# Loading 3 of the 32 rows of B's output weights second, by transfers of 119 and 9 partitions, and storing A's result by one transfer

## The chip, the cores and the metric

The kernel runs on one core of one Trainium2 chip. The metric is the device time of one execution in microseconds. Before the change the median of 3 runs is 825.41 us (825.28 to 825.46).

## What is computed

Two decode steps of attention with a key-value cache, A and B, are computed side by side and their outputs are set one behind the other. Each has one token, 32 heads of 128 and caches of 16384 positions in bfloat16. A attends to all positions, B only to the last 4096.

```python
W = min(4096, max(256, Sk // 4))                       # B only: window of the cache
q = (x @ wq).reshape(B, Sq, Hq, Dh).transpose(0, 2, 1, 3)
scores = einsum("bhqd,bhkd->bhqk", q, k) * Dh ** -0.5
p = softmax(scores, axis=-1)
o = einsum("bhqk,bhkd->bhqd", p, v)
out = o.transpose(0, 2, 1, 3).reshape(B, Sq, Hq * Dh) @ wo      # wo: 4096 x 512
# result: concatenate([out of A, out of B], axis=-1): 1 x 1 x 1024
```

Nearly all of the work is reading: the page counts 352.32 MB read from HBM, of which the two `wo` are 4 MB each.

## The kernel before, in words

**Tiles and order.** The caches are read in 20 tiles: 16 of A (two heads each, 128 partitions x 64 KB for keys and as much for values) and 4 of B (eight heads each, read as two halves of 32 KB a partition). A list `steps` (L94 to L101) puts B's tiles at T = 0, 7, 13 and 19. Keys go through a ring of two buffers (`kslot`), values through one buffer (`vslot`). For each tile VectorE multiplies the keys by the query (`scores_prod`, L206) and adds up along the head dimension (`scores_tree`, L212 and L216), ScalarE takes the exponentials (`soft`), TensorE multiplies by the values (`pv`, L272) and folds the result into a sum (`fold`, L288). The order is written out by hand (`manual_schedule`).

**Queues.** All large loads are issued by SyncE (SP), in program order, on one DMA queue (q1 in the profile). One such transfer of 128 partitions leaves 128 data packets, one a partition, and 16 packets of 4 bytes in the trace: each of the 16 DMA engines moves 8 partitions and then counts the transfer's semaphore up. Each engine works through its packets in the order of issue. SP also waits: before an issue it waits for the buffer to be free and, for some, for an older transfer to have landed.

**The end of the kernel.** In the last pass of the main loop (T = 19) the loads are the last values of B (`vlast`, two halves, L414 and L122) and then the two output weights (`load_wo`, L139 to L144), into the buffer `wot`: A's `wo` by one transfer, B's by five, of 16, 8, 4, 3 and 1 rows (`wo_pieces`, L368). A "row" here is one of the 32 rows of 512 numbers (1 KB) that each partition holds, so that a piece of n rows is 128 packets of n KB, and the pieces are 2048, 1024, 512, 384 and 128 KB.

TensorE then multiplies A's attention output by A's `wo` (`project_a`, L336), sums the groups (`finish_a`, L346), and ScalarE stores A's 512 numbers in two transfers (L350). `project_b` (L352 to L366) takes B's 32 rows in their order, r = 0 to 31, by four matmuls of 128 columns each (L357); every piece has a semaphore of its own, so the matmuls of a row wait until the piece that holds it has landed on all engines. When row 31 is done, VectorE copies the sums to `rows_b` (L362) and ScalarE and SP store them by four transfers (L364). Nothing is behind that but the end of the program.

Of the kernel before, what the change touches and what calls it, by code (L numbers as in the profile page):

```python
# [11 lines left out]
P = 128  # L12
# [4 lines left out]
HQ, DH = 32, 128  # L17
# [8 lines left out]
def kernel(  # L26
# [14 lines left out]
    nc = tc.nc  # L41
# [4 lines left out]
    DN = A_wo.shape[1]  # L46
# [16 lines left out]
    def kslot(name):  # L63
        return kring.tile([P, 2 * CH, DH], BF16, tag="kring", name=name)

    def vslot(name):
        return vring.tile([P, 2 * CH, DH], BF16, tag="vring", name=name)
# [7 lines left out]
    A, B = _Side(), _Side()  # L75
# [31 lines left out]
    def flat(t):  # L107
        return t.rearrange("p l d -> p (l d)")
# [15 lines left out]
    def new_k(T):  # L124
        K[T] = kslot("kt")

    def load_k(T, parts=(0, 1)):
        load(T, A_k_cache, B_k_cache, K[T], parts)

    def load_v(T, t):  # L130
        V[T] = t
        load(T, A_v_cache, B_v_cache, t)

    def load_wq(s):
        nc.sync.dma_start(  # L135
            out=s.wq_t.rearrange("p (c f) -> p c f", c=KC), in_=s.wq.rearrange("(p c) f -> p c f", c=KC)
        )

    def load_wo(s, pieces):  # L139
        src = s.wo.rearrange("(p r) f -> p r f", r=HQ)  # L140
        r = 0
        for n in pieces:
            nc.sync.dma_start(out=s.wo_t[:, r : r + n, :], in_=src[:, r : r + n, :])
            r += n  # L144

    def make_masks(s):
        nc.vector.tensor_reduce(out=s.mask[:, :], in_=by_head(s, identf[:, :]), axis=AX.X, op=ALU.add)
        z = QR - s.rows
        nc.vector.memset(s.fold[:, :], 0.0)
        nc.vector.tensor_reduce(  # L150
            out=s.fold[:, z : z + s.rows],
            in_=identf[:, :].rearrange("p (g x) -> p x g", g=NG)[:, 0 : s.rows, :], axis=AX.X, op=ALU.add,
        )

    def turn_x(xrow):
        ps = ps_t.tile([P, KC, 2], F32, tag="tp", name="xps")
        xr = xrow[:, :].rearrange("s (p c) -> s c p", c=KC)
        for c in range(KC):
            nc.tensor.matmul(ps[:, c, :], lhsT=xr[:, c, :], rhs=two_b[:, :], start=True, stop=True)
        for s in (B, A):  # L160
            nc.vector.tensor_copy(s.xT[:, :], ps[:, :, s.k])

    def clear_x(s, t):
        s.xb = t[:, 0 : s.nh * KC * P].rearrange("p (h c m) -> p h c m", h=s.nh, c=KC)
        nc.vector.memset(s.xb, 0.0)

    def spread_x(s):
        for j in range(s.nh):
            dst = s.xb[:, j, :, :]
            if s is A:  # L170
                dst = dst.rearrange("p c (h i) -> p c h i", h=s.nh)[:, :, j, :]
            else:
                dst = dst.rearrange("p c (i h) -> p c i h", h=s.nh)[:, :, :, j]
            nc.vector.tensor_copy(dst, s.xT[:, :].unsqueeze(2).broadcast_to([P, KC, P // s.nh]))

    def project_q(s):
        wq = s.wq_t.rearrange("p (c g h d) -> p c h g d", c=KC, h=s.nh, d=DH)
        for g in range(0, HQ // s.nh, 4):
            qp = ps_t.tile([P, 4, DH], F32, tag="tp", name="qp")
            n = KC * s.nh  # L180
            for k in range(n):
                c, j = divmod(k, s.nh)
                nc.tensor.matmul(  # L183
                    qp[:, :, :], lhsT=s.xb[:, j, c, :], rhs=wq[:, c, j, g : g + 4, :],
                    start=(k == 0), stop=(k == n - 1),
                )
            nc.scalar.copy(s.q[:, g : g + 4, :], qp[:, :, :])
# [14 lines left out]
    def scores_prod(T, u):  # L202
        s, g = steps[T]
        k = K[T][:, u * CH : (u + 1) * CH, :]
        j = g if s is A else 2 * g + u
        nc.vector.tensor_tensor(out=k, in0=k, in1=s.q[:, j : j + 1, :].broadcast_to([P, CH, DH]), op=ALU.mult)  # L206
# [23 lines left out]
    def max_all(T):  # L230
        un = tiles[T]
        s, U = un.s, un.s.units
        M = small.tile([2, 4], F32, tag="M", name="M")
        nc.vector.tensor_reduce(  # L234
            out=M[0:U, 0 : s.nh], in_=by_head(s, un.sm[0:U, 0:P]), axis=AX.X, op=ALU.max
        )
        Mr = one.tile([2, P], F32, tag="Mr", name="Mr")
        nc.vector.tensor_copy(  # L238
            by_head(s, Mr[0:U, :]), M[0:U, 0 : s.nh].unsqueeze(2).broadcast_to([U, s.nh, P // s.nh])
        )  # L240
        nc.tensor.transpose(un.sm[:, P : P + U], Mr[0:U, :], identf[0:U, 0:U])  # L241
# [77 lines left out]
    def own_o(s):  # L319
        s.own = square()  # L320
        pick_blocks(s.own[:, :], s.acc[:, :], DH, quad)
# [21 lines left out]
    def finish_a():  # L343
        ps = ps_m.tile([1, DN], F32, tag="sm", name="out_a")
        first = A.fold[:, QR - A.rows : QR - A.rows + 1]
        nc.tensor.matmul(ps[:, :], lhsT=first, rhs=A.wide[:, :], start=True, stop=True)  # L346
        row = one.tile([1, DN], BF16, tag="sc", name="row_a")
        nc.scalar.copy(row[:, :], ps[:, :])
        for f in range(0, DN, DN // 2):
            nc.scalar.dma_start(out=out[0, :, f : f + DN // 2], in_=row[:, f : f + DN // 2])  # L350

    def project_b():  # L352
        w = DN // NG
# [11 lines left out]
                out=out[0, :, DN + g * w : DN + (g + 1) * w], in_=rows[QR * g : QR * g + 1, :]  # L365
            )  # L366

    wo_pieces = (16, 8, 4, 3, 1)  # L368
    with tc.manual_schedule():
        xrow = one.tile([2, D], BF16, tag="pm", name="xrow")  # L370
        for s in (B, A):
            nc.scalar.dma_start(out=xrow[s.k : s.k + 1, :], in_=s.x[0, :, :])
        scratch = kslot("scratch")
        new_k(0)
        wqt = vslot("wqt")
        for k, s in enumerate((B, A)):
            s.wq_t = flat(wqt[:, k * CH : (k + 1) * CH, :])
        load_wq(B)
        load_k(0, (0,))
        load_wq(A)  # L380
        load_k(0, (1,))
        make_identity(nc, identf[:, :])
        nc.vector.tensor_copy(two_b[:, :], identf[0:2, 0:2])
        nc.vector.memset(ones[:, :], 1.0)
        nc.vector.tensor_reduce(
            out=quad[:, :], in_=identf[:, :].rearrange("p (m c) -> p c m", c=4), axis=AX.X, op=ALU.add
        )
        block = small.tile([P, P // 4], F32, tag="block", name="block", bufs=1)
        nc.vector.tensor_reduce(
            out=block[:, :], in_=identf[:, :].rearrange("p (m c) -> p m c", c=4), axis=AX.X, op=ALU.add  # L390
        )
        nc.vector.tensor_copy(
            fours[:, :].rearrange("p (m c) -> p m c", c=4), block[:, :].unsqueeze(2).broadcast_to([P, P // 4, 4])
        )
        clear_x(B, flat(scratch[:, :, :]))
        clear_x(A, one.tile([P, 2 * KC * P], BF16, tag="o4", name="xbA")[:, :])
        for o in o_banks:
            nc.vector.memset(o[:, :], 0.0)
        for s in (B, A):
            make_masks(s)  # L400
        turn_x(xrow)
        for s in (B, A):
            spread_x(s)
        project_q(B)
        project_q(A)
        new_k(1)
        load_k(1)
        for T in range(NT):
            if T >= 1:
                if T + 1 < NT:  # L410
                    new_k(T + 1)
                    load_k(T + 1)
                else:
                    load_v(T, kslot("vlast"))  # L414
            scores_prod(T, 0)
            if T >= 1:
                max_all(T - 1)
                soft(T - 1)
            scores_tree(T, 0)
            if T >= 1:  # L420
                for u in range(tiles[T - 1].s.units):
                    pv(T - 1, u)
                for u in range(tiles[T - 1].s.units):
                    fold(T - 1, u)
            if T + 1 < NT:
                load_v(T, vslot("vt"))
            else:
                wot = vslot("wot")
                for k, s in enumerate((A, B)):
                    s.wo_t = flat(wot[:, k * CH : (k + 1) * CH, :]).rearrange("p (r f) -> p r f", r=HQ)  # L430
                load_wo(A, (HQ,))
                load_wo(B, wo_pieces)
            scores_prod(T, 1)
            scores_tree(T, 1)
            tile_max(T)
        max_all(NT - 1)
        soft(NT - 1)
        normalize(A)
        own_o(A)
        pv(NT - 1, 0)  # L440
        spread_o(A)
        pv(NT - 1, 1)
        for u in range(2):
            fold(NT - 1, u)
        normalize(B)
        own_o(B)
        project_a()
        spread_o(B)
        finish_a()
        project_b()  # L450

# [29 lines left out]
```

## Time and profile before

| | |
|---|---|
| median of 3 runs | 825.41 us |
| the profiled execution: its own time | 825.65 us |
| its span (first to last instruction on the core) | 823.9 us |
| outside the span | 1.75 us |
| busy: VectorE / TensorE / ScalarE | 766.4 / 184.5 / 61.4 us |
| HBM read | 352.32 MB, 428 GB/s over the span |

The span is cut by the page into 40 slices of 20.6 us. Its row of the DMA engines' busy share shows "9", that is 90% or more, in 39 slices and "7" in the last one. Under "queue" the page lists q1 (the loads of SP and two of the last stores), q10 (ScalarE's small transfers) and two queues of kind "instruction", q8 and q14, by which the engines' own programs are read during the run. A busy share of DMA in a stretch is a mean over the 16 engines: 0.25 can be read as four of the 16 at work. The trace also keeps a record of each single packet (start, duration, size, queue); packets of one engine follow one another without a gap, which allows the 16 engines to be followed through the run.

### The profile page before, as it was taken

What the parts mean: (1) busy time and instruction counts of PE and PEld (TensorE: products, weight loads), DVE (VectorE), ACT (ScalarE), POOL (GpSimd) and SP (SyncE); (2) the same over time, 40 slices, a digit from 0 to 9 for tenths busy, and PEclk for the clock granted to TensorE, in tenths of its full rate; (3) what the DMA queues carried; (4) which work ended last, traced back from release to release, by engine and by line L of the source; (5) the groups of instructions that cost most, each with busy time, mean ns of one, the idle gap of its engine ahead of it and who ended that gap; (6) DMA issues with size and microseconds to landing.
All of it is one profiled execution on the core that took longest, in us unless ns stands there. A gap on an engine that the chain in (4) does not pass through costs nothing.

```text
span 823.9 us, 3928 instructions
## 1 busy us (share of the span) xinstructions
PE 184.5 (22%) x1606; PEld 60.9 (7%) x1606; DVE 766.4 (93%) x348; ACT 61.4 (7%) x165; POOL 0.7 (0%) x6
## 2 busy tenths in 40 slices
PE   3402312213030303220303112030402030303037
PEld 1100000001010001000000001010100010101012
DVE  2899899999999999999999999999999998999992
ACT  0102000001010000100000001010200000000011
POOL 0000000000000000000000000000000000000000
PEclk9755556565665656555656565555656565656568
DMA  9999999999999999999999999999999999999997
GB/s 384 434 431 435 449 420 449 426 437 433 430 436 430 422 441 439 414 449 427 439 423 443 420 445 413 453 417 428 435 449 420 452 418 442 427 422 441 423 429 292
DMA packets 8097, 352.57 MB, mean 428 GB/s; under 512 B 908, under 2 KB 1040, under 8 KB 1296
## 3 DMA queue, kind: packets, MB, share of 16 engines
q1 hardware_dynamic: 8068, 352.33, 99.2%
q8 instruction: 12, 0.20, 0.1%
q14 instruction: 5, 0.04, 0.0%
q10 hardware_dynamic: 12, 0.00, 0.0%
HBM read 352.32 MB, written 0.00 MB: 428 GB/s over the span
## 4 chain that ended last, share of the span: by engine, by line
DMA 56%; DVE 43%; issue 0%; SPq 0%; PE 0%; DVEq 0%
DMA kt<-in_A_k_cache_dram 44%; DVE kt L206 20%; DVE kt L212 20%; DMA kt<-in_B_k_cache_dram 5%; DMA vlast<-in_B_v_cache_dram 4%; DMA wot<-in_B_wo_dram 4%; DVE sc L216 3%; DVE Mr L238 0%; DVE M L234 0%; SPq L135 0%; SPq L122 0%; PE out_b L357 0%; DVE rows_b L362 0%; DVEq L216 0%
## 5 line engine op out<-in xcount | busy, mean ns | idle before, releaser
L212 DVE TENSOR_TENSOR kt<-kt 128x8192 bf16<-128x8192 bf16 (+3 forms) x160 | 345.0, 2156 | 4.8
L206 DVE TENSOR_TENSOR kt<-kt,qA 128x16384 bf16<-128x16384 bf16 x32 | 278.0, 8687 | 13.2 <-DMA kt<-in_A_k_cache_dram 13.2
L272 PE MATMUL o<-vt,pm 128*8 128x512 bf16 (+1 forms) x1216 | 113.9, 553 | 181.7 <-DMA vt<-in_A_v_cache_dram 161.1
L206 DVE TENSOR_TENSOR kt<-kt,qB 128x16384 bf16<-128x16384 bf16 x8 | 69.5, 8684 | 14.1 <-DMA kt<-in_B_k_cache_dram 14.1
L228 PE MATMUL sm<-identf,m 128*1 128x128 f32 (+1 forms) x20 | 7.4, 371 | 235.2 <-DVE m L224 235.2
L272 PEld LDWEIGHTS <-pm 128*8 128x8 bf16 (+1 forms) x1280 | 39.9, 114 | 253.2 <-issue 206.8
L216 DVE TENSOR_REDUCE sc<-kt 128x128 f32<-128x1024 bf16 x40 | 48.8, 1220 | 2.7
L241 PE MATMUL sm<-identf,Mr 1*128 1x1 f32 (+1 forms) x20 | 5.2, 261 | 178.5 <-DVE Mr L238 178.5
L247 ACT ACTIVATE bias<-sm 128x1 f32<-128x1 f32 (+1 forms) x20 | 3.4, 172 | 447.3 <-PE sm L241 447.3
L285 ACT COPY o<-o 128x512 f32<-128x512 f32 x24 | 14.1, 587 | 264.6 <-PE o L272 233.8
L228 PEld LDWEIGHTS sm<-identf,m 128*1 128x1 f32 (+1 forms) x20 | 1.6, 79 | 252.4 <-issue 241.2
L288 PE MATMUL accA<-o,foldA 128*32 128x512 f32 x32 | 16.7, 605 | 11.1 <-ACT o L285 11.1
L241 PEld LDWEIGHTS sm<-identf,Mr 1*128 1x128 f32 (+1 forms) x20 | 3.5, 176 | 184.9 <-DVE Mr L238 184.9
L260 ACT ACTIVATE pm<-p,maskA 128x256 bf16<-128x256 bf16 x32 | 14.5, 502 | 0.5
L183 PE MATMUL qp<-wqt,xbA 128*128 128x512 bf16 x32 | 9.4, 465 | 10.6 <-DMA wqt<-in_A_wq_dram 10.6
L253 ACT ACTIVATE p<-sc,bias 128x256 bf16<-128x256 f32 (+1 forms) x24 | 11.3, 472 | 0.6
L288 PE MATMUL accB<-o,foldB 128*32 128x512 f32 x16 | 9.9, 709 | 2.7 <-ACT o L285 2.7
L260 ACT ACTIVATE pm<-p,maskB 128x128 bf16<-128x128 bf16 x32 | 10.3, 392 | 0.3
L183 PE MATMUL qp<-wqt,scratch 128*128 128x512 bf16 x32 | 8.9, 447 | 5.0 <-DMA wqt<-in_B_wq_dram 5.0
L224 DVE TENSOR_REDUCE m<-sc 128x1 f32<-128x256 f32 (+1 forms) x20 | 8.4, 420 | 0.7
L272 PE MATMUL o<-vlast,pm 128*16 128x512 bf16 x64 | 6.1, 552 | 1.6 <-ACT pm L260 1.6
L234 DVE TENSOR_REDUCE M<-sm 1x2 f32<-1x128 f32 (+1 forms) x20 | 5.4, 271 | 0.6 <-PE sm L228 0.6
(60 smaller groups left out, 52.9 us busy)
## 6 DMA issues: line engine op xcount, KB each, us to landing
kt<-in_B_k_cache_dram SPq DMA_DIRECT2D x8, 4096.0 KB, 30.0
vt<-in_B_v_cache_dram SPq DMA_DIRECT2D x6, 4096.0 KB
vlast<-in_B_v_cache_dram SPq DMA_DIRECT2D x2, 4096.0 KB, 39.2
wqt<-in_B_wq_dram SPq DMA_DIRECT2D x1, 4096.0 KB, 12.5
wqt<-in_A_wq_dram SPq DMA_DIRECT2D x1, 4096.0 KB
wot<-in_A_wo_dram SPq DMA_DIRECT2D x1, 4096.0 KB
wot<-in_B_wo_dram SPq DMA_DIRECT2D x1, 2048.0 KB
wot<-in_B_wo_dram SPq DMA_DIRECT2D x1, 1024.0 KB
```

Source lines behind the costliest of these rows:

```text
L183: nc.tensor.matmul(qp[:, :, :], lhsT=s.xb[:, j, c, :], rhs=wq[:, c, j, g : g + 4, :], start=(k == 0), stop=(k == n - 1),)
L206: nc.vector.tensor_tensor(out=k, in0=k, in1=s.q[:, j : j + 1, :].broadcast_to([P, CH, DH]), op=ALU.mult)
L212: nc.vector.tensor_tensor(out=k[:, :, 0:w], in0=k[:, :, 0:w], in1=k[:, :, w : 2 * w], op=ALU.add)
L216: nc.vector.tensor_reduce(out=tiles[T].sc[:, u * CH : (u + 1) * CH], in_=k[:, :, 0:8], axis=AX.X, op=ALU.add)
L224: nc.vector.tensor_reduce(out=m[:, 0:U], in_=un.sc[:, :].rearrange("p (u n) -> p u n", u=U), axis=AX.X, op=ALU.max)
L228: nc.tensor.transpose(un.sm[0:U, 0:P], m[:, 0:U], identf[:, :])
L241: nc.tensor.transpose(un.sm[:, P : P + U], Mr[0:U, :], identf[0:U, 0:U])
L253: nc.scalar.activation(out=un.part(p, u), in_=un.part(un.sc, u), func=ACT.Exp, scale=inv, bias=bias[:, u : u + 1], accum_out=s.cs[:, col + ...
L260: nc.scalar.activation(out=un.pm[u][:, :, j, :], in_=un.part(p, u).rearrange("p (i c) -> p i c", c=4), func=ACT.Copy, scale=s.mask[:, j : ...
L272: nc.tensor.matmul(o[r0 : r0 + rows, :], lhsT=un.pm[u][:, i, :, :].rearrange("p a b -> p (a b)"), rhs=V[T][:, u * un.n + 4 * i : u * un.n ...
L285: nc.scalar.copy(osb[:, :], un.o[u][:, :])
L288: nc.tensor.matmul(s.acc[QR * q : QR * (q + 1), :], lhsT=s.fold[:, (per - 1 - off) * rows : (per - 1 - off) * rows + QR], rhs=osb[:, :], s ...
```

## The change

B's pieces are now 16, 3, 8, 4 and 1 rows, so that the 3-row piece, rows 16 to 18, is second and not fourth. It is loaded by two transfers, one of partitions 0 to 118 and one of 119 to 127. All other pieces stay transfers of 128 partitions. SP issues seven transfers for `wot` in place of six. A's result goes out by one transfer of 512 numbers in place of two of 256. No instruction of TensorE or VectorE changes, nor the order in which `project_b` takes the rows.

```diff
-        for n in pieces:
-            nc.sync.dma_start(out=s.wo_t[:, r : r + n, :], in_=src[:, r : r + n, :])
+        for n, cuts in pieces:
+            for a, b in zip((0,) + cuts, cuts + (P,)):
+                nc.sync.dma_start(out=s.wo_t[a:b, r : r + n, :], in_=src[a:b, r : r + n, :])
             r += n
...
-        for f in range(0, DN, DN // 2):
-            nc.scalar.dma_start(out=out[0, :, f : f + DN // 2], in_=row[:, f : f + DN // 2])
+        nc.scalar.dma_start(out=out[0, :, 0:DN], in_=row[:, :])
...
-    wo_pieces = (16, 8, 4, 3, 1)
+    wo_pieces = ((16, ()), (3, (119,)), (8, ()), (4, ()), (1, ()))
...
-                load_wo(A, (HQ,))
+                load_wo(A, ((HQ, ()),))
                 load_wo(B, wo_pieces)
```

## The prediction

> **What bounds the kernel now.** I read the page's chain of work first, then its last 60 us in order of time.
>
> ```profile
> DMA 56%; DVE 43%; issue 0%; SPq 0%; PE 0%; DVEq 0%
> ```
>
> ```profile
> 761.25 30.10 DMA vlast<-in_B_v_cache_dram
> 791.35 0.02 issue
> 791.37 29.14 DMA wot<-in_B_wo_dram
> 820.51 0.04 issue
> 820.55 0.56 PE out_b L357 x16
> 821.12 0.02 issue
> 821.14 0.29 DVE rows_b L362
> ```
>
> The columns are start, duration and what. The last 60 us are two loads, then 0.56 us of matmuls, a copy and the stores: the end is set by the landing of B's `wo`. VectorE's share (43%) lies ahead of that. Then TensorE's and VectorE's rows of the timeline in this stretch (start, duration, engine, line; in brackets the idle time before and who ended it):
>
> ```profile
> 818.26 0.63 PE L357 MATMUL out_b<-wot,OpB 128*32 128x128 bf16 x32 [0.36 <-DMA wot<-in_B_wo_dram]
> 819.51 0.41 PE L357 MATMUL out_b<-wot,OpB 128*32 128x128 bf16 x16 [0.62 <-DMA wot<-in_B_wo_dram]
> 820.55 0.54 PE L357 MATMUL out_b<-wot,OpB 128*32 128x128 bf16 x16 [0.63 <-DMA wot<-in_B_wo_dram]
> 821.14 0.29 DVE L362 CAST rows_b<-out_b 128x128 bf16<-128x128 f32 x1 [4.37 <-PE out_b L357]
> ```
>
> TensorE waits for the pieces of 8, 4 and 3 rows one after the other; single records show the four matmuls of the 1-row piece at 820.855. So what counts is when the last DMA engine has the last piece. The table by stretches (start:end, length, busy time of each engine; read the last two columns, the DMA engines' mean share and GB/s):
>
> ```profile
> 816.00:816.50 0.50, 0.50 (x2) 0.00 (x0) 0.45 (x2) 0.00 (x0) 0.00 (x0) 1.00 0.99 393
> 816.50:817.00 0.50, 0.26 (x13) 0.18 (x16) 0.23 (x2) 0.38 (x1) 0.00 (x0) 1.00 0.84 326
> 817.00:817.50 0.50, 0.50 (x48) 0.50 (x40) 0.00 (x0) 0.19 (x1) 0.00 (x0) 1.00 0.62 244
> ...
> 818.50:819.00 0.50, 0.39 (x28) 0.25 (x17) 0.00 (x0) 0.00 (x0) 0.00 (x0) 1.00 0.27 107
> 819.00:819.50 0.50, 0.00 (x0) 0.00 (x0) 0.00 (x0) 0.00 (x0) 0.00 (x0) 1.00 0.25 94
> 819.50:820.00 0.50, 0.41 (x16) 0.26 (x16) 0.00 (x0) 0.00 (x0) 0.00 (x0) 1.00 0.18 66
> 820.00:820.37 0.37, 0.00 (x0) 0.00 (x0) 0.00 (x0) 0.00 (x0) 0.00 (x0) 1.00 0.07 22
> ```
>
> Shares times 16: all 16 engines work at 816.0, some 9 at 817.5, four from 818.5 on, one at 820.2. The engines had equal bytes but don't end together. Followed through the packet records, the 16 end the last piece at 816.54 plus 0, 0.21, 0.28, 0.35, 0.36, 0.55, 0.76 (**seven early ones**), 1.56, 1.61, 1.69, 1.70, 1.92, and 3.17, 3.19, 3.50, 3.83 us (820.37). They are never idle; a lag, once there, stays. It comes from the reads of program code:
>
> ```profile
> q8 instruction: 12, 0.20, 0.1%
> q14 instruction: 5, 0.04, 0.0%
> ```
>
> Each of q8's packets (16 KB) throws one engine back by 1.55 us, in turn over eight engines, three of which are hit twice before the end (lags 3.19, 3.50, 3.83); q14's five (8 KB) cost 0.7 to 0.97 us each, three of them the same engine (3.17). The mean lag is 1.54, so that bytes spread to suit would end at 818.1: 2.3 us is all that is to be had here.
>
> **The change part by part.**
>
> *The split of the 3-row piece.* A 3 KB packet takes 0.121 us from start to start on every engine; eight and their semaphore packet took the latest engine 0.974 us (819.038 to the next piece's first packet at 820.012). Where do 119 + 9 packets go? No transfer of such a width is in the trace. The rows there: 128 partitions give 8 packets on each of 16 engines, one partition (the two loads of x) one packet on one engine. Equal shares, on as many engines as allow them, fit both; for 119 = 7 x 17 that is seven engines with 17 each, for 9 nine engines with one each. Which seven, the trace doesn't tell either, but the one-partition loads sit between the packets of an early engine (lag 0.28). Bounds for the latest engine: from -0.97 us (it gets none) to 18 - 8 = 10 packets more, +1.21, with a second semaphore packet +1.22 us. I take none, the end to which the one known row (a narrow transfer on an early engine) is nearer.
>
> Three sentences on this from the Trainium skill, which the sum does without: its page DMA: Bandwidth & Descriptors (section "Why a DMA increments its semaphore by 16 and not by 1") says that a transfer runs on the largest number of engines up to 16 that divides its slowest dimension, and, issued from SP, on the lowest-numbered of them. By it 119 is seven engines (0 to 6) and 9 is engines 0 to 8; the trace agrees for 128 and for 1, no run yet shows 119. Seven is also the count of early engines, though the trace has no numbers on them.
>
> Then: the latest engine ends at 820.367 - 0.974 = 819.39. The seven early ones get 10 packets more, +1.22: the latest of them ends at 816.54 + 0.76 + 1.22 = 818.52, out of the way by 0.87 us. An engine of the middle gets one packet or none and ends earlier. If a single packet goes to the latest engine, the gain is 7 x 0.121 = 0.85.
>
> *The order.* Rows 16 to 18 land by 811.47 (the first engine's end of the 16-row piece) + 0.76 + 18 x 0.121 + 0.46 (semaphore packet at 820.358, seen at 820.814) = 814.9, before TensorE begins B at 816.82: no wait of theirs. The latest engine's 8- and 4-row pieces came ahead of the 3-row one and don't move: TensorE begins them at 818.26 and 819.51 as before, and starts the last of the 16 matmuls of the 4-row piece at 819.70. The 1-row piece then is seen at 820.814 - 0.974 = 819.84, its matmuls start at 819.88 in place of 820.855. What was hidden, 0.18 us between the two groups, stays; next in line is the 4-row piece.
>
> *SP.* One issue more, 0.33 to 0.43 us by the rows of L143. In the changed instruction list the waits for `vlast`'s halves stand before the 4-row and the 1-row piece (before: 3-row and 1-row, issued at 791.37 and 801.105). So the last issue is again at 801.1, and the first engine needs it at 816.08: 15 us of older packets hide it. Behind it on SP are only the stores of 821.46. Cost 0; beyond 15 us each late us would be one.
>
> *A's store.* One issue of ScalarE (0.26 us) is gone, between 817.2 and 821.47, when it has nothing else to do: 0. Two packets of 26 ns become one of some 46 ns, on an early engine that may now still be busy: under 0.06 us, not on the last engine.
>
> *Sum.* -0.97 us; the copy, stores and 1.75 us outside the span stay. From the profiled execution: 825.65 - 0.97 = 824.68. The median of the runs is 0.24 lower: 825.41 - 0.97 = **824.4 us**.
>
> **The rivals.**
>
> *The limit is where the bytes are written, not the engine (slower).* Every engine runs at the same 27.0 GB/s (32 KB in 1.213 us), whatever it reads. If that is the pace at which one group of partitions takes data, and each engine so far had a group of its own, then the latest engine's group gets the same 8 x 3 KB from others, which take turns with it: 0.97 won, 0.97 lost. And the seven early engines send 18 packets at half pace, 18 x 0.242 = 4.36 in place of 0.97: they end at 819.9 to 820.7, and up to 0.97 later where their own groups take others' 8 packets as well, 821.7. It decides from the point where these pass 820.37. That is 0 to +1.3 us; I take the middle: **826.1 us**. For it: the equal pace of all engines, and that they are all busy when the piece comes (share 0.98 from 812 to 816). Against it: nothing in the trace has two engines on one group, and a limit of the engine fits as well. The Trainium skill speaks for this rival: SBUF — State Buffer, section "Door 1: The DMA port swizzle", gives 16 write ports by groups of partitions and 27.6 GB/s measured for partitions 0 to 3 alone; by that the change would bring nothing. No run here shows it yet.
>
> *The seven are not the early ones (slower).* With one of the four latest among them the end moves by +0.56 (lag 3.17) to +1.22: up to **826.6**. An engine must lag by over 2.61 for it to be slower than now; four do. For it: the trace has no numbers on the engines. Against: the one-partition loads' engine is early.
>
> *The change doesn't shift the load.* If shares needn't be equal, 119 go on 15 or 16 engines by 8 and 7, and 9 on nine: each has 7 to 9 as before, -0.12 to +0.13 us: **825.4**.
>
> *All 119 on one engine.* 120 x 0.121 - 0.97 = 13.6 us more for an engine that ended at 816.82: the end at 830.4, +10: **835.4**. For it: the one-partition loads did so. Against: equal shares of 17 are possible.
>
> **How the numbers follow.** Forecast 0.42, place of writing 0.30, not the early ones 0.13, no shift 0.07, one engine 0.03, something not thought of 0.05. A measurement of this kernel can tell 0.2%, 1.65 us, from no change. No case gains that (the forecast's end is -0.97): faster 0.01. Beyond +1.65 lie one engine (0.03), half of the unknown (0.02) and a tail of the place of writing (0.02): slower 0.07, same 0.92. The range goes from the forecast with the runs' spread, 824.2, to 826.4, which holds the place of writing and half of the wrong-engine case: about 0.83. The forecast's own range is 824.2 to 824.8; the signs are nearly even, so it stands here.
>
> **What would show it.** Right: 17 or 18 packets of 3 KB in a row on seven engines at 0.121 us each, four late ends up to 819.4, the last matmul group at 819.88, a span of 822.9. The place of writing: packets of 3 KB at 0.2 us and more, and 8 KB packets of late engines beside them longer than 0.313. Wrong engines: a long run of 3 KB on one that ends last. The forecast fails also if the code reads fall on other engines in other executions.

## The result and the profile after

The changed kernel takes 828.75 us (median of 6 runs, 828.44 to 829.02) against 825.40 us (825.22 to 825.56) for the kernel before on the same chip: a ratio of 1.0041, 95% interval 1.0028 to 1.0054. It is slower by 3.35 us, beyond the range of the forecast. The profiled execution takes 828.75 us with a span of 826.9 us, 3.0 us more than before.

The chain of work that ended last has the same members as before, start, duration and what:

```profile
760.92 30.12 DMA vlast<-in_B_v_cache_dram
...
791.05 32.34 DMA wot<-in_B_wo_dram
...
823.43 0.75 PE out_b L357 x20
...
824.21 0.29 DVE rows_b L362
```

`vlast` lands as before, 0.3 us earlier in this execution. The landing of B's `wo` takes 32.3 in place of 29.1 us, and that is the loss. TensorE's part of it, from the timeline (start, duration, then the idle time before and who ended it):

```profile
817.42 1.08 PE L357 MATMUL out_b<-wot,OpB 128*32 128x128 bf16 x64 [2.25 <-DMA wot<-in_B_wo_dram]
819.79 0.51 PE L357 MATMUL out_b<-wot,OpB 128*32 128x128 bf16 x12 [1.28 <-DMA wot<-in_B_wo_dram]
822.14 1.05 PE L357 MATMUL out_b<-wot,OpB 128*32 128x128 bf16 x32 [1.85 <-DMA wot<-in_B_wo_dram]
823.43 0.72 PE L357 MATMUL out_b<-wot,OpB 128*32 128x128 bf16 x20 [0.24 <-DMA wot<-in_B_wo_dram]
```

These are, in order, the pieces of 16, 3, 8 and 4 + 1 rows (64, 12, 32 and 20 matmuls). TensorE now waits for each of them: even the 16-row piece, which is ahead of the cut one in the queue, is awaited until 817.42, and the cut piece until 819.79.

How busy the DMA engines are, and what they move, shows where the time goes. These are rows of the table by stretches; read the last two columns (mean share of the 16 engines, GB/s). First the kernel before, then the changed one:

```profile
811.40:813.50 2.10, 1.88 (x16) 0.77 (x20) 0.45 (x3) 0.17 (x1) 0.00 (x0) 1.00 0.97 406
813.50:816.00 2.50, 2.24 (x32) 0.81 (x20) 1.75 (x6) 0.59 (x1) 0.00 (x0) 1.00 0.96 395
```

```profile
811.40:813.50 2.10, 2.01 (x34) 0.85 (x33) 1.71 (x6) 0.00 (x0) 0.00 (x0) 1.00 1.03 309
813.50:816.00 2.50, 1.51 (x4) 0.47 (x5) 1.19 (x5) 1.16 (x2) 0.00 (x0) 1.00 1.00 230
```

The engines count as busy nearly all the time in both (a share a little over 1.00 comes from records that overlap by some ns), but from 813.5 to 816 they move 230 in place of 395 GB/s. The single packets have become longer. Their durations from the packet records, in ns:

| packet | before: median / longest | changed kernel: median / longest |
|---|---|---|
| 16 KB | 614 / 621 | 614 / 1145 |
| 8 KB | 313 / 324 | 455 / 624 |
| 3 KB (the cut piece) | 125 / 132 | 208 / 275 |

The records also show where the cut piece went. Runs of 17 packets of 3 KB, and then one more, begin on seven engines, single packets on two (and none on seven), as equal shares of 119 and 9 have it. Each engine's run begins where its 16-row piece ends, so that its lag can be read: the seven begin at 811.48, 811.60, 812.10, 812.35, at 813.64, 813.76, and at 816.27. So four early engines, two of the middle and **one of the four latest** carry 18 packets; two early ones got one packet, one early one none. The latest of the seven ends last of all, at 823.26 (before, the last end was 820.37). The engine with the loads of x is among the seven. The reads of program code fall on the engines in the same pattern as before.

The engine that ends last shows the loss in parts. By its three reads of program code on q14 it is the engine that had the lag 3.17 and ended at 819.71 in the kernel before; now it ends 3.55 us later. Its first three 16 KB packets take the usual 0.61 to 0.62 us, but the last five, which run while other engines already write the cut piece, take 0.68 to 1.15, so that its 16-row piece ends at 816.26 in place of 814.63: 1.63 us are lost before its own part of the cut piece begins. Its 18 packets of 3 KB then take 2.87 us in place of 0.97 for 8: 1.90 us more, of which 10 packets at the old 0.121 are 1.21. Its other packets keep their old pace.

### The profile page after: what moved, and what is told of

The parts are those of the page before. It is cut to its first block, busy times and chain, and to the rows that moved or that the text cites. A ratio compares the mean times of both kernels' runs of the same rounds, so it can differ in the third digit from the quotient of the medians.

```text
span 826.9 us, 3928 instructions
## 1 busy us (share of the span) xinstructions
PE 185.0 (22%) x1606; PEld 61.3 (7%) x1606; DVE 766.4 (93%) x348; ACT 61.5 (7%) x165; POOL 0.7 (0%) x6
## 4 chain that ended last, share of the span: by engine, by line
DMA 56%; DVE 43%; issue 0%; SPq 0%; PE 0%; DVEq 0%
DMA kt<-in_A_k_cache_dram 44%; DVE kt L207 20%; DVE kt L213 20%; DMA kt<-in_B_k_cache_dram 5%; DMA wot<-in_B_wo_dram 4%; DMA vlast<-in_B_v_cache_dram 4%; DVE sc L217 3%; DVE Mr L239 0%; DVE M L235 0%; SPq L135 0%; PE out_b L357 0%; SPq L122 0%; DVE rows_b L362 0%; DVEq L217 0%
```

## The experiments

Two causes were at hand. The first is **the place of writing**, a rival in the prediction: engines that write the same group of partitions share its pace, and a narrow transfer (one of fewer than 128 partitions) makes engines write where others write. The second is **the wrong engines**: 10 packets more for an engine that is late already. Besides, the order of the pieces, the number of transfers and A's store had to be excluded. All ratios are to the kernel before on the same chip, with 95% intervals.

### e1_order: the order alone

```diff
-    wo_pieces = ((16, ()), (3, (119,)), (8, ()), (4, ()), (1, ()))
+    wo_pieces = ((16, ()), (3, ()), (8, ()), (4, ()), (1, ()))
```

> The 3-row piece second, but by one transfer of 128 partitions; A's store single as in the changed kernel. If the loss comes from the place of the writes (two engines writing one group of partitions share its pace) or from load put on engines that are late already, nothing of it is left: 8 packets on each engine, 0.121 us each, 825.4 us (825.1 to 825.7). If the order of the pieces costs, it stays at 828 to 829.

Measured: 825.51 us, ratio 1.0003 (0.9993 to 1.0012). The order costs nothing.

### e2_half: narrow transfers, but no load shifted

```diff
+    wo_pieces = ((16, ()), (3, (64,)), (8, ()), (4, ()), (1, ()))
```

> The 3-row piece second, cut at 64 instead of 119: two transfers of 64 partitions. By equal shares each engine still has 8 packets of 3 KB (4 and 4), so that no load is shifted. Shifted load as the cause: 825.4 (825.1 to 825.8). Place of the writes as the cause: 16 engines write 64 partitions at a time, the 3 KB packets take well over 0.121 us and the end moves by +0.5 to +2, 826 to 827.5.

Measured: 828.28 us, ratio 1.0035 (1.0022 to 1.0048): +2.94 us, above the +2 that was expected at most from the place. The packet records show 4 and 4 packets of 3 KB on the engines; these have a median of 198 ns, the 8 KB packets 486 (longest 889). The stretches of this kernel:

```profile
811.40:813.50 2.10, 2.10 (x34) 0.93 (x34) 1.67 (x6) 0.00 (x0) 0.00 (x0) 1.00 1.03 284
813.50:816.00 2.50, 1.51 (x4) 0.47 (x5) 1.22 (x6) 1.16 (x2) 0.00 (x0) 1.00 1.00 259
```

No engine has more to do than before, and still 259 GB/s are moved in place of 395. The shifted load is not needed for the loss.

### e3_late: the cut piece in fourth place

```diff
+    wo_pieces = ((16, ()), (8, ()), (4, ()), (3, (119,)), (1, ()))
```

> The cut of 119 and 9 kept, but the piece back in its old place, fourth. Shifted load alone: the end is that of the late engine among the seven, lag 3.17 + 10 x 0.121, +0.6 us, 826.0, as it would be in second place. Place of the writes: the seven write across the others here too, but the pieces before land undisturbed: +1.5 to +3.5, 827 to 829. Order as the cause: 826 or less.

Measured: 827.84 us, ratio 1.0030 (1.0019 to 1.0041): +2.5 us. The cut costs there too, 0.85 us less than in second place. All packets of 16 KB keep their 621 ns at most; 8 KB packets go up to 554.

### e4_store: A's store alone

```diff
     # the kernel before, with
-        for f in range(0, DN, DN // 2):
-            nc.scalar.dma_start(out=out[0, :, f : f + DN // 2], in_=row[:, f : f + DN // 2])
+        nc.scalar.dma_start(out=out[0, :, 0:DN], in_=row[:, :])
```

> The kernel before with A's store as one transfer, nothing else. All theories: no change, 825.4 (825.2 to 825.6).

Measured: 825.46 us, ratio 1.0000 (0.9991 to 1.0010). The store does nothing to the time.

### e5_none, e6_xdram, e7_xsbuf: load and place apart

In all three B's pieces are whole, in the old order, and SP issues them from the second piece on behind VectorE's last tile. The second and third have one more copy of 119 packets of 3 KB, second in the queue, which puts 17 packets on each of seven engines: once into HBM, once into partitions.

```diff
             tile_max(T)
+            if T + 1 == NT:
+                nc.sync.dma_start(out=TARGET, in_=B.wo.rearrange("(p r) f -> p r f", r=HQ)[0:119, 16:19, :])
+                load_wo(B, wo_pieces[1:], 16)
# e5_none: without the copy;  e6_xdram: TARGET = spare[0:119, :, :], a tensor in HBM
# e7_xsbuf: TARGET = partitions 0 to 118 of K[T], 3 KB each
```

> Control for the next two: the kernel before with A's store single, and SP's issues of B's pieces from the second on moved behind VectorE's last tile (some 799 us, 12 us before the first engine needs them). All theories: 825.4 (825.2 to 825.7).

Measured: 825.46 us, ratio 1.0002 (0.9992 to 1.0011).

> The control and an extra copy, second in the queue, that the result doesn't use: 119 partitions' shares of rows 16 to 18 (3 KB each) from HBM to HBM. It gives the seven engines 17 packets more each and writes nothing to the partitions. All pieces of B go by 128 partitions. If an engine's load is all that counts, the late one of the seven (lag 3.17 before) gets 17 x 0.121 = 2.06 more and ends at 821.8: +1.4, 826.8 (826.4 to 827.5, later if a packet to HBM takes longer, by its own record). Place of the writes: the same, and the other engines' packets keep 0.313 (8 KB) and 0.614 us (16 KB).

Measured: 827.00 us, ratio 1.0019 (1.0010 to 1.0029): +1.54 us against the control. The last engine ends at 821.63 (821.8 expected), with a run of 17. The copied packets have a median of 121 ns, the 16 KB and 8 KB packets of all engines keep 621 and 324 ns at the most. The stretches:

```profile
811.40:813.50 2.10, 2.00 (x34) 0.83 (x23) 1.51 (x5) 0.41 (x1) 0.00 (x0) 1.00 0.93 386
813.50:816.00 2.50, 1.69 (x47) 0.79 (x50) 1.18 (x5) 0.75 (x2) 0.00 (x0) 1.00 1.00 412
```

> The same extra copy of 119 x 3 KB, but into 119 partitions of a key buffer that is done with (the result doesn't use it either). Load of the engines alone: as with the copy to HBM, +1.4, 826.8. Place of the writes: on top of that what the cut piece cost without shifted load (+2.5 to +3), 829 to 831, and 8 KB packets of 0.4 to 0.6 us.

Measured: 830.04 us, ratio 1.0058 (1.0041 to 1.0075): +4.58 us against the control and +3.04 against the same copy into HBM. The 8 KB packets have a median of 475 ns (longest 788).

By equal shares the same seven engines read the same bytes in both. Writing them to HBM lengthens no other packet: 412 GB/s in the stretch. So a transfer that runs on seven engines, or the reading of its bytes, doesn't slow the others by itself. Writing them into partitions costs 3 us more. So both causes exist, and the larger one is the place.

### e8_one: the cut on the smallest piece

```diff
+    wo_pieces = ((16, ()), (8, ()), (4, ()), (3, ()), (1, (119,)))
```

> The cut of 119 and 9 on the last piece of 1 row instead of the 3-row piece (order 16, 8, 4, 3, 1). Place of the writes: in proportion to the bytes a third of the loss of the piece cut in fourth place (2.5), +0.8, 826.2 (825.8 to 826.8); less if most engines are through by then. Shifted load alone: 10 packets of 0.043 on the late engine of the seven, -0.2 us against the latest engine, 825.4 or a little less.

Measured: 825.97 us, ratio 1.0007 (0.9998 to 1.0017): +0.66 us by the medians, near the 0.8 of the place, but its interval holds no change.

### e9_more: as many transfers, but wide

```diff
+    wo_pieces = ((16, ()), (1, ()), (2, ()), (8, ()), (4, ()), (1, ()))
```

> The 3-row piece second, in two transfers of 1 and 2 rows, both of 128 partitions: as many transfers as in the changed kernel, as many bytes, and each engine still writes its usual partitions. If it is the narrow transfers' writes across the engines, nothing is lost but 8 packets' fixed part, some 0.06 us: 825.5 (825.2 to 825.8). If one transfer more is what costs: 828.

Measured: 825.47 us, ratio 1.0002 (0.9993 to 1.0012). One transfer more costs nothing while each engine writes its usual partitions.

### e10_probe: the place looked at directly, first try

```diff
             tile_max(T)
+            if T + 1 == NT:
+                lone = A.wo.rearrange("(p r) f -> p (r f)", r=HQ)
+                flat_k = K[T][:, :, :].rearrange("p l d -> p (l d)")
+                nc.sync.dma_start(out=flat_k[0:4, 0:12288], in_=lone[0:4, 0:12288])
+                nc.sync.dma_start(out=flat_k[0:16:4, 12288:22528], in_=lone[0:16:4, 0:10240])
+                nc.sync.dma_start(out=flat_k[0:128:32, 22528:30720], in_=lone[0:128:32, 0:8192])
```

> The kernel before with A's store single, and behind its last piece three extra loads of 4 partitions each, one packet an engine, which the result doesn't use: 24 KB into partitions 0 to 3, then 20 KB into 0, 4, 8, 12, then 16 KB into 0, 32, 64, 96. Only the packets' durations count, not the time. If a place takes 27 GB/s whoever writes, and neighbouring partitions share a place: about 3.6 us each for the first four (0.9 if each engine goes at its own pace), 0.76 for the second four, if these are four places. For the third four 0.61 if they are four places and 1.2 if they share by twos, as the Trainium skill has it (SBUF — State Buffer, section Door 1: The DMA port swizzle). If engines have their own pace wherever they write: 0.90, 0.76, 0.61.

Measured: 1.298, 1.646, 2.001 and 1.308 us for 24 KB; 1.134, 1.189, 0.759 and 1.002 for 20 KB; 0.831, 0.820, 0.644 and 0.614 for 16 KB. This decides nothing: the packets of the first load begin up to 3.1 us apart, as their engines end B's pieces, so that the packets of one load met those of the next and of B's last pieces. The next run has one load at a time with nothing else on the queues.

### e11_alone: the place looked at directly, one load at a time

```diff
         project_b()
+        lone = A.wo.rearrange("(p r) f -> p (r f)", r=HQ)
+        flat_b = B.wo_t.rearrange("p r f -> p (r f)")
+        nc.sync.dma_start(out=flat_b[0:1, :], in_=lone[0:1, :])
...
+        nc.sync.dma_start(out=flat_b[0:128:32, :], in_=lone[0:128:32, :])
# the eight rows of partitions, L453 to L460: 0:1, 0:2, 0:4, 0:8, 0:16:4, 0:64:32, 0:128:64, 0:128:32
```

> The kernel before with A's store single, and behind its end eight loads that the result doesn't use, each waiting for the one before it, of 32 KB per partition: partition 0 alone; 0 and 1; 0 to 3; 0 to 7; then 0, 4, 8, 12; 0 and 32; 0 and 64; 0, 32, 64, 96. One packet a partition, each on an engine of its own, nothing else on the queues; only the packets' durations count. Alone a packet takes 1.2 us. If engines have a pace of their own wherever they write, all take 1.2 us. If four neighbouring partitions share a place of 27 GB/s: two packets about 2.4, four 4.8, eight 4.8 us (two places), 0, 4, 8, 12 again 1.2. 0 and 32, and 0, 32, 64, 96: 2.4 if the place is shared as the Trainium skill has it (SBUF — State Buffer, section Door 1: The DMA port swizzle), else 1.2; 0 and 64: 1.2 either way.

This is one execution. Each load waits for the one before it, so SP's list of waits gives the time from a load's issue to its landing. A line names the load that waited, so its number belongs to the load one line above it in the program (L454 waits for the load of L453, L486 for the last):

```profile
SPq L456 <- DMA wot<-in_A_wo_dram: 5.9, 1, 5.9
SPq L457 <- DMA wot<-in_A_wo_dram: 5.8, 1, 5.8
SPq L459 <- DMA wot<-in_A_wo_dram: 4.0, 1, 4.0
SPq L455 <- DMA wot<-in_A_wo_dram: 4.0, 1, 4.0
SPq L486 <- DMA wot<-in_A_wo_dram: 3.8, 1, 3.8
SPq L458 <- DMA wot<-in_A_wo_dram: 3.1, 1, 3.1
SPq L460 <- DMA wot<-in_A_wo_dram: 3.0, 1, 3.0
SPq L454 <- DMA wot<-in_A_wo_dram: 2.6, 1, 2.6
```

| partitions of the load | wait, us | durations of its 32 KB packets, us |
|---|---|---|
| 0 | 2.6 | 1.66 |
| 0, 1 | 4.0 | 2.23, 2.23 |
| 0 to 3 | 5.9 | 3.10 to 3.74 |
| 0 to 7 | 5.8 | 3.15 to 3.71 |
| 0, 4, 8, 12 | 3.1 | 1.55 to 1.77 |
| 0, 32 | 4.0 | 2.15, 2.32 |
| 0, 64 | 3.0 | 1.53, 1.93 |
| 0, 32, 64, 96 | 3.8 | 1.91 to 2.25 |

Four packets into 0 to 3 take twice as long as four into 0, 4, 8 and 12, and 0 with 32 is as slow as 0 with 1, while 0 with 64 is not. That is what the place theory asks for: four neighbouring partitions and those 32 further on share a place, which takes less than its writers can send. In these loads the rows read from HBM change along with the partitions written, so that this run alone doesn't tell a shared place of writing from one of reading; the two copies above do, for the stream. The map is that of the Trainium skill, page SBUF — State Buffer, section "Door 1: The DMA port swizzle (why `[64,N]` ≈ `[32,N]`)". The pace is not the one expected: four packets (131072 bytes, from the first start to the last end 3.77 us) are 34.7 GB/s, above the 27.0 of a single engine in the stream, not equal to it. The 27.6 GB/s that this page of the Trainium skill gives for partitions 0 to 3 (at 1 MiB) are not what this load shows, and the measurement decides here.

## Why the prediction was wrong, point by point

- **What bounds the kernel**: right. The landing of B's `wo` set the end before and after, and the 16 engines end at times apart by the reads of code.
- **The split into shares**: right in number. 119 went on seven engines by 17, 9 on nine by one (the rule of the Trainium skill, DMA: Bandwidth & Descriptors, "Why a DMA increments its semaphore by 16 and not by 1", agrees). **Wrong in whose**: "I take none, the end to which the one known row (a narrow transfer on an early engine) is nearer". The one known row, that a one-partition load's engine is early, said nothing of the other six: two are of the middle, one is among the four latest. That was the second rival; by its arithmetic it alone is +0.56 us (lag 3.17), and its way of working out was borne out by the copy into HBM (17 packets: end at 821.8 expected, 821.63 measured). So the gain of 0.97 us could not have come even at the old price of a packet.
- **The price of a 3 KB packet, "0.121 us from start to start on every engine"**, and the price of the packets beside it, which the sum left as they were: the step that failed most. The row is of packets that each engine writes into its usual partitions. In the cut piece they took 0.208 us (median), and the 8 KB packets 0.455 in place of 0.313. This was the first rival, but sized too small: 0 to +1.3 us, where the cut without any shifted load cost 2.94 (e2_half) and the writes into partitions 3.04 (e7_xsbuf against e6_xdram). The rival's bound charged each group of partitions once for the foreign bytes and let it work on at full pace. Measured, the total falls to 230 to 309 GB/s from 811.4 to 816. A reason that fits is that an engine held up at another's group leaves its own group without bytes; no run here shows which packet waits for which, so that this stays argued.
- **One rival or another**: the cases were taken one by one, each with its own price. Two held at once. Added up, 0.56 (load) + 2.94 (place, e2_half) = 3.5 us, against 3.35 measured. That these agree so closely is in part chance: e2_half cuts at 64 and not at 119, so that all 16 engines carry its cut piece.
- **"no wait of theirs", of the matmuls of rows 16 to 18**: wrong for the same reason. TensorE waited for them until 819.79. The wait for the 16-row piece until 817.42 was a part that no case had: pieces ahead of the cut one are hit where late engines still work on them (16 KB packets up to 1.145 us), which on the engine that ends last is 1.63 of its 3.55 us. It is in line with this that the loss is smaller in fourth place (e3_late, 2.5), where all 16 KB packets stay at 0.621.
- **The order, SP's issue, A's store, the number of transfers**: right, each costs nothing (ratios 1.0003, 1.0002, 1.0000, 1.0002 in e1_order, e5_none, e4_store, e9_more).
- **The chances**: by the prediction's own mark of 1.65 us, +3.35 is slower, to which it gave 0.07, and no change 0.92. That rested on the too small bound of the place. The first rival, at 0.30, pointed the right way; its time of 826.1 was too low by 2.65 us.

## What to carry to other kernels

Loads into fewer than 128 partitions can slow the wide loads beside them, not only themselves (2.94 us for a piece of 384 KB in e2_half): look at GB/s beside the DMA share, since engines whose packets take longer still count as busy. Before load is moved between DMA engines, find out by a small copy which engines a shape uses and whether the late ones are among them, and measure the copy once into HBM and once into the partitions to have load and place apart. When two rivals don't exclude each other, the range has to hold their sum.

## What the runs showed of the hardware

- Groups of partitions behave as shared places: 0 to 3 together, 0 with 32, but not 0 with 4, 8, 12 or 64 (e11_alone). Packets of 32 KB took 3.1 to 3.7 us for four partitions of one place and 1.55 to 1.77 us for four of four places. In the stream it is the writing that counts (e7_xsbuf against e6_xdram, 3.04 us).
- A copy of 119 x 3 KB between two places in HBM ran beside the full stream of loads at 121 ns a packet and slowed no other packet (e6_xdram).
- TensorE's granted clock was 0.50 from 820 us on in the changed kernel and 1.00 from 820 to 822 before; the last matmuls took up to 0.314 in place of 0.229 us. By the clock's records the full clock lasted 13.65 us in both, from 806.16 and from 808.87, so that TensorE's longer waits are not shown to be the reason: e9_more has 0.50 from 820 to 821 as well, and no loss. From the last landing packet to `rows_b` it is 0.95 us (824.21 - 823.26) in place of 0.77 (821.14 - 820.37), about 0.2 of the 3 us; the slower clock and the matmuls of the 4-row piece, which now stand right ahead of the last four, are not told apart in it.
